# A transformer block on one core: queries of the last two blocks with tokens on partitions, attention later, and small products and memsets ahead of the first real work

## The chip, the cores and the metric

The kernel runs on one core of a Trainium2 chip. The metric is device time in microseconds (us), as the median of several runs. A profile of one execution gives each instruction's start and duration; times in it count from the start of its span.

## The reference, cut to what matters

Input and output are 2048 tokens of 512 numbers in bf16.

```python
def _layernorm(x, axis=-1, eps=1e-5):
    ...
def _A_ref(x, wqkv, wo):                       # 32 heads of 16
    q, k, v = ...                              # x @ wqkv
    phi = lambda t: jnp.where(t > 0, t + 1, jnp.exp(t)) + 1e-6
    pq, pk = phi(q), phi(k)
    kv = jnp.einsum("bhsd,bhse->bhde", pk, v)
    z = jnp.einsum("bhsd->bhd", pk)
    num = jnp.einsum("bhqd,bhde->bhqe", pq, kv)
    den = jnp.einsum("bhqd,bhd->bhq", pq, z)[..., None] + 1e-6
    o = num / den
    return (...)(o).reshape(B, S, D) @ wo
def _B_ref(x, w1, w2):                         # w1: 512 x 1792, w2: 1792 x 512
    ...                                        # relu(x @ w1) @ w2
h = x + _A_ref(_layernorm(x, axis=-1), A_wqkv, A_wo)
h2 = h + _B_ref(_layernorm(h, axis=-1), B_w1, B_w2)
```

## The kernel before

The 2048 tokens are 16 tiles of 128 (t = 0 to 15), and four blocks of four tiles (c = 0 to 3). Nothing is looped: one list of words, `ORDER`, is walked from front to back, and each word calls a function `op_<name>` with the numbers behind it. So the list sets the order of the instructions on every engine; the framework adds the waits (an instruction that reads or overwrites what another wrote waits for that one's semaphore, also where both run on the same engine). All loads, transposes by DMA and stores are issued by SP, one after the other, over eight semaphores in turn.

The words that matter here:

- `lx`, `lk`, `lq`, `lv`, `lo`, `l1`, `l2`: loads of the input and of the weights. `const`, `masks`, `table`: constants, masks, ACT's function table.
- `S.t`, `A.t` (DVE): mean and variance of tile t, in two instructions (BN_STATS, BN_AGGR). `R.t.n` (ACT): the scale, as a logarithm and an exponential, for n tiles. `N.t` (DVE): the normalized tile.
- `T.t` (PE) and `E.t` (ACT): transpose of tiles 0 to 3 by PE, and its copy to `lnT`. `X.t` (SP): the same for the others by DMA.
- `K.t` (PE, four products): keys of a tile. `F`, `U` (ACT: exponential, relu), `M`, `D` (DVE: minimum, sum): the function phi on them. `W`, `qW`: sum and relu in one DVE instruction instead. `G.t` (PE, four products): the sum over tokens of the normalized tile times its keys, from which `kv` makes the state with the value weights `wv`; `m` multiplies it by `wo`.
- `za`, `zf`, `z`, `zc`, `zh`: z, the sum of the keys.
- `Q.c.j` (PE, four products): queries of a block with features on partitions, a quarter at a time; `qF`, `qU`, `qM`, `qD` the function phi.
- `dn.c` (PE, 16 products of 8 columns): the denominators of a block; `dnl`, `dnx` (ACT): their reciprocals, spread over 16 columns each; `dt` (DMA) or `rt` with `re`/`rv`: the transposes of those; `dm.c.j` (DVE): queries times reciprocals, into `pqs`.
- `h.t` (PE, four products) and `hD.t` (DVE): the attention's output and the residual sum; `s`, `a`, `r`, `n`, `x`/`t` with `e`: the second layer norm and its transpose.
- `p.c.f` (PE, four products, w1), `pA`/`pD` (relu on ACT or DVE, two f at a time, into `at`), `f.t` (PE, 14 products, w2), `fo.t` (DVE), `fd.t` (store): the second layer. A number in these words that names a bank is the PSUM bank written.
- `warm`, `warmf`: products of zeros, ahead of and between the first transposes.

Of the kernel before, what the change touches and what calls it, by code (L numbers as in the profile page):

```python
# [18 lines left out]
const lx.0.1 lx.1.1 warmf.4.3 warm.1.3 S.0 table A.0 R.0.1 S.1 lx.2.2 lk.0.2 warm.1.3 N.0 A.1 S.2 R.1.1 lk.2.2  # L19
lx.4.2 A.2 T.0.7 E.0 warm.1.3 S.3 R.2.1 K.0.1.0.2 lx.6.2 A.3 R.3.1 K.0.1.2.2 N.1 T.1.5 F.0.1 E.1 N.2 N.3 T.3.2  # L20
lx.8.4 E.3 S.4 S.5 A.4 T.2.5 lx.12.4 lq.0.2 A.5 K.1.0.0.2 R.4.2 S.6 M.0.1 N.5 S.7 N.4 X.5 E.2 U.0.1 D.0.1 K.3.7
K.1.0.2.2 F.3.1 M.3.1 X.4 K.2.3.0.2 U.3.1 A.7 A.6 K.2.3.2.2 U.1.1 R.6.2 F.2.1 F.1.1 G.0 D.3.1 G.3 S.9 U.2.1 N.7
N.6 S.8 K.5.1 K.4.0 M.2.1 A.8 A.9 R.8.2 U.4.2 M.1.1 X.7 D.2.1 F.4.2 D.1.1 N.9 S.12 X.6 N.8 X.9 G.2 K.7.3 S.13
A.12 A.13 G.1 R.12.2 K.6.2 K.9.1 M.4.2 S.10 F.6.2 N.12 D.4.2 S.11 A.10 U.6.2 X.8 M.6.2 N.13 G.4 X.12 K.8.0 A.11
R.10.2 S.14 D.6.2 G.5 G.6 X.13 N.10 N.11 S.15 F.8.2 M.8.2 X.11 A.15 U.8.2 A.14 D.8.2 R.14.2 G.7 za.2 za.4 K.12.0
G.9 K.13.1 N.15 N.14 X.10 lq.2.2 K.11.3 F.12.2 K.10.2 M.12.2 U.12.2 F.10.2 masks X.15 X.14 lv.0.2 lv.2.2 l1.0.2
U.10.2 za.6 D.12.2 M.10.2 G.8 za.8 D.10.2 Q.0.1.1 Q.0.0.0 qF.0.0.2 qU.0.0.2 za.10 G.12 K.14.2 K.15.3 Q.0.2.0
za.12 Q.0.3.1 G.13 F.14.2 G.11 qF.0.2.2 l2.10.4 qM.0.0.2 M.14.2 W.14.2 zf.12 G.10 qD.0.0.2 qM.0.2.2 G.14
# [28 lines left out]
def kernel(  # L57
# [10 lines left out]
    nc = tc.nc  # L68
# [45 lines left out]
    erep = const.tile([P, P], BF16, name="erep")  # L114
# [9 lines left out]
    z_sb = big.tile([P, KD], F32, name="z_sb")  # L124
    acts = [big.tile([P, KF, CW], BF16, name=f"at{i}") for i in range(2)]
# [15 lines left out]
    r4 = rd  # L141
# [19 lines left out]
    unit = {"k": 0, "q": NT}  # L161
# [49 lines left out]
    op_l2 = lambda k, n: load_d(w2_sb, w2_v, k, n)  # L211

# [139 lines left out]
    op_W = lambda t, n: relu_add_of("k", t, n)  # L352
    op_qF = lambda c, j, n: exp_of("q", c * KD + j, n)
# [23 lines left out]
    def op_z(jb, b, t0=0):  # L377
        at_bank["z"] = b
        parts = [pk(t)[:, 0, :] for t in range(t0, NT)] + [acts[1][:, i, :] for i in (4, 5) if t0]
        for i, part in enumerate(parts):  # L380
            nc.tensor.matmul(
                bk[:, b, jb : jb + 1], lhsT=part[:, jb * P : (jb + 1) * P], rhs=ones[:],
                start=(i == 0), stop=(i == len(parts) - 1),
            )
# [39 lines left out]
    def op_d4(c, b):  # L424
        at_bank["d4", c] = b
        for jb in range(KD):
            nc.tensor.matmul(
                bk[jb * Q4 : (jb + 1) * Q4, b, :], lhsT=zhd[:, jb, :], rhs=pqT[c][:, jb, :],
                start=True, stop=True,
            )  # L430

    def op_dl4(c):
        nc.scalar.activation(
            out=ld[:, c % 2, :], in_=bk[:, at_bank["d4", c], :], func=ACT.Ln, bias=eps6[:], scale=1.0
        )

    def op_dx4(c):
# [154 lines left out]
```

## Time and profile before

| | |
|---|---|
| median of three runs | 170.3 us (169.92 to 170.45) |
| span of the profiled execution | 168.8 us; its own device time is not listed beside it |
| PE / DVE / ACT busy | 163.1 / 104.4 / 65.1 us |
| bytes moved by DMA | 15.49 MB, 92 GB/s over the span |
| granted TensorE clock | 1.000 on the mean |

The span runs from the first to the last instruction, and the median of the runs is 1.5 us above it. In the rows, a line such as L237 is a line of the kernel, "x4" counts instructions merged into a row, and what stands in brackets is the idle time ahead and what ended it. The profile gives PE's matmuls with their length through the pipeline, so that neighbours overlap; what one costs is the distance from start to start.

### The profile page before, as it was taken

What the parts mean: (1) busy time and instruction counts of PE and PEld (TensorE: products, weight loads), DVE (VectorE), ACT (ScalarE), POOL (GpSimd) and SP (SyncE); (2) the same over time, 40 slices, a digit from 0 to 9 for tenths busy, and PEclk for the clock granted to TensorE, in tenths of its full rate; (3) what the DMA queues carried; (4) which work ended last, traced back from release to release, by engine and by line L of the source; (5) the groups of instructions that cost most, each with busy time, mean ns of one, the idle gap of its engine ahead of it and who ended that gap; (6) DMA issues with size and microseconds to landing.
All of it is one profiled execution on the core that took longest, in us unless ns stands there. A gap on an engine that the chain in (4) does not pass through costs nothing.

```text
span 168.8 us, 2286 instructions
## 1 busy us (share of the span) xinstructions
PE 163.1 (97%) x855; PEld 78.0 (46%) x871; DVE 104.4 (62%) x205; ACT 65.1 (39%) x97; POOL 4.8 (3%) x21
## 2 busy tenths in 40 slices
PE   7989999999999999999999999999999999999993
PEld 5344344445644454444444444444444444444553
DVE  3899998997668999699819879215102432050251
ACT  3698775875879947432000003004320420400000
POOL 7400000000000000000000000000000000000000
PEclk9999999999999999999999999999999999999999
DMA  4975575689533353534130015500320000002023
GB/s 112 352 245 97 97 66 124 176 270 378 174 64 65 77 138 87 134 62 95 37 62 0 31 31 122 126 4 0 62 93 0 31 0 4 0 0 93 0 65 94
DMA packets 30491, 15.49 MB, mean 92 GB/s; under 512 B 23184, under 2 KB 29328, under 8 KB 30480
## 3 DMA queue, kind: packets, MB, share of 16 engines
q1 hardware_dynamic: 30480, 15.34, 35.5%
q8 instruction: 7, 0.11, 0.3%
q14 instruction: 4, 0.03, 0.1%
HBM read 7.86 MB, written 2.10 MB: 59 GB/s over the span
## 4 chain that ended last, share of the span: by engine, by line
PE 85%; DVE 7%; DMA 4%; issue 1%; SPq 0%
PE bk L541 29%; PE bk L521 28%; PE bk L505 8%; PE bk L318 8%; PE bk L362 6%; PE bk L310 4%; DVE st L237 3%; DMA x_nat<-in_A_x_dram 2%; DMA lnT<-h_nat 2%; DVE h_nat L262 2%; PE bk L459 1%; DVE eb L335 1%; PE bk L403 1%; PE bk L415 1%; SPq L201 0%
## 5 line engine op out<-in xcount | busy, mean ns | idle before, releaser
L541 PE MATMUL bk<-w_sb,at 128*128 128x512 bf16 (+2 forms) x247 | 50.1, 355 | 0.3
L521 PE MATMUL bk<-lnT,w_sb 128*128 128x512 bf16 x219 | 50.0, 379 | 0.3
L527 ACT ACTIVATE at<-bk 128x1024 bf16<-128x1024 f32 x14 | 14.2, 1023 | 57.4 <-PE bk L521 57.4
L541 PEld LDWEIGHTS <-at 128*128 128x128 bf16 x252 | 23.6, 98 | 25.4 <-ACT at L527 0.3
L549 DVE SCALAR_TENSOR_TENSOR gT<-bk,rstd,h_nat 128x512 bf16<-128x512 f32 (+2 forms) x18 | 12.2, 689 | 35.7 <-PE bk L541 35.6
L521 PEld LDWEIGHTS <-w_sb 128*128 128x128 bf16 x224 | 21.8, 98 | 25.8
L532 DVE TENSOR_SCALAR at<-bk 128x1024 bf16<-128x1024 f32 x14 | 17.1, 1218 | 12.8 <-PE bk L521 12.6
L328 ACT ACTIVATE eb<-bk 128x1024 bf16<-128x1024 f32 (+1 forms) x18 | 16.6, 928 | 6.6 <-PE bk L310 4.8
L310 PE MATMUL bk<-wk_sb,lnT 128*128 128x512 bf16 x63 | 15.3, 380 | 0.4 <-ACT lnT L291 0.3
L505 PE MATMUL bk<-m_sb,pqs 128*128 128x512 bf16 x63 | 15.4, 380 | 0.1
L318 PE MATMUL bk<-lnT,wq_sb 128*128 128x512 bf16 x61 | 15.1, 379 | 0.1
L362 PE MATMUL bk<-at,h_nat 128*128 128x512 bf16 x55 | 13.5, 379 | 0.1
L331 ACT ACTIVATE rb<-bk 128x1024 bf16<-128x1024 f32 (+1 forms) x14 | 12.5, 904 | 0.3 <-PE bk L310 0.3
L511 DVE TENSOR_TENSOR h_nat<-bk,x_nat 128x512 bf16<-128x512 f32 x16 | 10.5, 680 | 2.9 <-PE bk L505 2.9
L237 DVE BATCH_NORM_STATS2 st<-x_nat 128x6 f32<-128x512 bf16 x16 | 10.8, 680 | 2.4 <-DMA x_nat<-in_A_x_dram 2.4
L239 DVE BATCH_NORM_STATS2 st<-h_nat 128x6 f32<-128x512 bf16 x16 | 10.7, 683 | 0.1
L310 PEld LDWEIGHTS <-lnT 128*128 128x128 bf16 x64 | 6.0, 98 | 8.4 <-ACT lnT L291 1.0
L362 PEld LDWEIGHTS <-h_nat 128*128 128x128 bf16 x64 | 6.2, 98 | 7.4 <-issue 0.2
L505 PEld LDWEIGHTS <-pqs 128*128 128x128 bf16 x64 | 5.9, 98 | 7.9 <-DVE pqs L495 1.8
L318 PEld LDWEIGHTS <-wq_sb 128*128 128x128 bf16 x64 | 5.9, 98 | 6.4
L472 ACT ACTIVATE wk_sb<-ld 128x1024 bf16<-128x1024 f32 x8 | 8.1, 1050 | 0.1
L335 DVE TENSOR_SCALAR eb<-eb 128x1024 bf16<-128x1024 bf16 (+1 forms) x18 | 6.8, 383 | 0.9 <-ACT eb L328 0.9
(63 smaller groups left out, 93.5 us busy)
## 6 DMA issues: line engine op xcount, KB each, us to landing
out_dram<-gT SPq DMA_DIRECT2D x15, 128.0 KB, 1.9
w_sb<-in_B_w_dram SPq DMA_DIRECT2D x2, 896.0 KB, 9.8
x_nat<-in_A_x_dram SPq DMA_DIRECT2D x2, 512.0 KB, 6.3
w_sb<-in_B_w_dram SPq DMA_DIRECT2D x2, 512.0 KB, 9.5
x_nat<-in_A_x_dram SPq DMA_DIRECT2D x3, 256.0 KB, 4.6
w_sb<-in_B_w_dram SPq DMA_DIRECT2D x2, 384.0 KB, 3.5
wk_sb<-in_A_wqkv_dram SPq DMA_DIRECT2D x2, 256.0 KB, 4.3
wq_sb<-in_A_wqkv_dram SPq DMA_DIRECT2D x2, 256.0 KB, 4.9
```

Source lines behind the costliest of these rows:

```text
L237: op_S = lambda t: nc.vector.bn_stats(out=st[:, t, :], in_=x_nat[:, t, :])
L310: nc.tensor.matmul(bk[:, b, :], lhsT=lnT[c][:, kd, j * P : (j + 1) * P], rhs=wk_sb[:, kd, :], start=(kd == 0), stop=(kd == KD - 1),)
L318: nc.tensor.matmul(bk[:, b, :], lhsT=wq_sb[:, kd, j * P : (j + 1) * P], rhs=lnT[c][:, kd, :], start=(kd == 0), stop=(kd == KD - 1),)
L328: nc.scalar.activation(out=buf(eb, kind, i, n), in_=bank(at_bank[kind, i], n), func=ACT.Exp)
L331: nc.scalar.activation(out=buf(rb, kind, i, n), in_=bank(at_bank[kind, i], n), func=ACT.Relu)
L362: nc.tensor.matmul(bk[:, KD + kd, :], lhsT=ln_nat[:, t, kd * P : (kd + 1) * P], rhs=pk(t)[:, 0, :], start=(t == 0), stop=(t == NT - 1),)
L505: nc.tensor.matmul(bk[:, b, :], lhsT=pqs[:, (c * KD + jb) % NQ, j * P : (j + 1) * P], rhs=m_sb[:, jb, :], start=(jb == 0), stop=(jb == KD ...
L521: nc.tensor.matmul(bk[:, b, cols], lhsT=w1_sb[:, kd, f * P : (f + 1) * P], rhs=lnT[c][:, kd, cols], start=(kd == 0), stop=(kd == KD - 1),)
L527: nc.scalar.activation(out=acts[c % 2][:, f : f + n, :], in_=bank(at_bank["p", c, f], n), func=ACT.Relu)
L532: nc.vector.tensor_scalar(out=acts[c % 2][:, f : f + n, :], in0=bank(at_bank["p", c, f], n), scalar1=0.0, scalar2=None, op0=ALU.max,)
L541: nc.tensor.matmul(bk[:, b, 0 : w * P], lhsT=acts[c % 2][:, f, j * P : (j + 1) * P], rhs=w2_sb[:, f, k * P : (k + w) * P], start=(f == 0), ...
L549: nc.vector.scalar_tensor_tensor(out=o_t[:, t % NO, cols], in0=bk[:, at_bank["f", t, k], 0 : w * P], scalar=rstd2[:, t : t + 1], in1=h_nat ...
```

## The change

The queries of tiles 8 to 15 (blocks 2 and 3) are now made with tokens on partitions (`Y.t`, 4 products each; `yF`, `yU`, `yM`, `yD` for phi). For them the denominators come from DVE: z is spread to all partitions by four products of 128 columns with ones (`zd` on DVE, `zr` on PE, `zC` on ACT), `dT` multiplies two tiles by it into an f32 tile, `dR` adds up 16 columns at a time; `dl`, `dx` (ACT) make the reciprocals, `dy` (DVE) multiplies, and `ty` (DMA) transposes into `pqs`. Their `h` products come later, between the first `f` and `p.1`. Four of the `p.0` blocks are computed in two halves of 256 columns.

At the start, `warmf` is replaced by `warms.70`, seventy products of 64 columns, and 40 memsets of one column of a new tile `pad` (`idle.24`, then twice `idle.8`) stand on DVE. The loads up to `lq` head the list, `masks` comes ahead of `const`, and loads of `w2` are spread among the transposes. The mask `erep` and unused functions go.

```diff
-const lx.0.1 lx.1.1 warmf.4.3 warm.1.3 S.0 table A.0 R.0.1 S.1 lx.2.2 lk.0.2 warm.1.3 N.0 A.1 S.2 R.1.1 lk.2.2
+lx.0.1 lx.1.1 lx.2.2 lk.0.2 lk.2.2 lx.4.2 lx.6.2 lx.8.4 lx.12.4 lq.0.2 table masks const S.0 A.0 S.1 R.0.1 A.1 N.0 S.3
+idle.24 R.1.1 S.2 A.3 A.2 N.1 R.3.1 N.3 R.2.1 N.2 S.5 idle.8 idle.8 S.4 A.5 A.4 warms.70.2 T.0.3 warm.1.4 warm.1.7
+T.1.0 T.3.4 warm.1.5 E.0 E.1 E.3 R.4.2 T.2.5 K.0.7.0.2 K.0.7.2.2 K.1.3.0.2 K.3.0 F.0.1 E.2 K.1.3.2.2 K.2.2.0.2
...
+    pad = const.tile([P, 1], F32, name="pad")
-    ones = const.tile([P, 1], BF16, name="ones")
+    ones = const.tile([P, P], BF16, name="ones")
...
+    def op_idle(n):
+        for _ in range(n):
+            nc.vector.memset(pad[:], 0.0)
...
+    def op_Y(t, b):
+        c, j = divmod(t, CT)
+        at_bank["y", t] = b
+        for kd in range(KD):
+            nc.tensor.matmul(
+                bk[:, b, :], lhsT=lnT[c][:, kd, j * P : (j + 1) * P], rhs=wq_sb[:, kd, :],
+                start=(kd == 0), stop=(kd == KD - 1),
+            )
...
+    def op_zr(b):
+        at_bank["zr"] = b
         for jb in range(KD):
             nc.tensor.matmul(
...
+                bk[:, b, jb * P : (jb + 1) * P], lhsT=ones[:], rhs=zdg[:, jb, :], start=True, stop=True
+            )
...
+    def op_dT(t, n):
+        nc.vector.tensor_tensor(
+            out=prod[:, 0:n, :], in0=toks(t, n), in1=zrep.broadcast_to([P, n, D]), op=ALU.mult
+        )
+
+    def op_dR(t, n):
+        nc.vector.tensor_reduce(
+            out=den[:, t * H : (t + n) * H], in_=prod[:, 0:n, :].rearrange("p t (h r) -> p (t h) r", r=DH),
+            axis=mybir.AxisListType.X, op=ALU.add,
+        )
...
+    def op_dy(t, n):
+        nc.vector.tensor_tensor(out=toks(t, n), in0=toks(t, n), in1=rn[:, t % CT : t % CT + n, :], op=ALU.mult)
...
+    def op_ty(t):
+        nc.sync.dma_start_transpose(out=pqs_of(t), in_=toks(t, 1)[:, 0, :])
```

What this makes of the order shows at three places. First DVE at the start, before: from the normalization of tile 0 (L262) to the statistics of tiles 2 and 3 (L237, L238) and on to the normalizations of tiles 1 to 3. The brackets name the semaphores an instruction waits for; DVE_49 is DVE's own.

```order
L262 TENSOR_SCALAR h_nat<-x_nat,mv,rstd 128x512 [waits DVE_49,Activation_49]
L238 BN_AGGR mv<-st 128x2 [waits DVE_49]
L237 BN_STATS st<-x_nat 128x6 [waits DMAHW2_49]
L238 BN_AGGR mv<-st 128x2 [waits DVE_49]
L237 BN_STATS st<-x_nat 128x6
L238 BN_AGGR mv<-st 128x2 [waits DVE_49]
L262 TENSOR_SCALAR h_nat<-x_nat,mv,rstd 128x512 [waits Activation_49] x2
```

And after, from the same normalization (now L264) through tile 3's statistics (L239), the memsets (L213) and tile 2's statistics to tile 5's and the second row of memsets:

```order
L264 TENSOR_SCALAR h_nat<-x_nat,mv,rstd 128x512 [waits Activation_49]
L239 BN_STATS st<-x_nat 128x6 [waits DMAHW2_49]
L213 MEMSET pad 128x1
L213 MEMSET pad 128x1 [waits DVE_49] x23
L239 BN_STATS st<-x_nat 128x6
L240 BN_AGGR mv<-st 128x2
L240 BN_AGGR mv<-st 128x2 [waits DVE_49]
L264 TENSOR_SCALAR h_nat<-x_nat,mv,rstd 128x512 [waits Activation_49]
L264 TENSOR_SCALAR h_nat<-x_nat,mv,rstd 128x512 [waits DVE_49,Activation_49] x2
L239 BN_STATS st<-x_nat 128x6 [waits DMAHW5_49]
L213 MEMSET pad 128x1
L213 MEMSET pad 128x1 [waits DVE_49] x15
```

The second statistics of the pair now stand behind 24 memsets, of which 23 wait for DVE's own semaphore, and those of tile 4 behind 16.

Second, ACT at the start, before: the scales (L243, L244) of tiles 0 and 1, the copy of tile 0's transpose (L291), the scales of tiles 2 and 3, the exponential of tile 0's keys (L328) and the copies of the other two.

```order
L243 ACTIVATE rstd<-mv,eps_73 128x1 [waits DVE_49]
L244 ACTIVATE rstd<-rstd 128x1 [waits Activation_49]
L291 ACTIVATE lnT_81<-bk 128x4x128 [waits PE_49]
L243 ACTIVATE rstd<-mv,eps_73 128x1 [waits DVE_49]
L244 ACTIVATE rstd<-rstd 128x1 [waits Activation_49]
L243 ACTIVATE rstd<-mv,eps_73 128x1 [waits DVE_49]
L244 ACTIVATE rstd<-rstd 128x1 [waits Activation_49]
L328 ACTIVATE eb<-bk 128x512 [waits PE_49]
L291 ACTIVATE lnT_81<-bk 128x4x128 [waits PE_49] x2
```

And after, from the scale of tile 3 on (L245, L246; copies L293, exponential L339):

```order
L245 ACTIVATE rstd<-mv,eps_73 128x1 [waits DVE_49]
L246 ACTIVATE rstd<-rstd 128x1 [waits Activation_49]
L245 ACTIVATE rstd<-mv,eps_73 128x1 [waits DVE_49]
L246 ACTIVATE rstd<-rstd 128x1 [waits Activation_49]
L293 ACTIVATE lnT_81<-bk 128x4x128 [waits PE_49] x3
L245 ACTIVATE rstd<-mv,eps_73 128x2 [waits DVE_49]
L246 ACTIVATE rstd<-rstd 128x2 [waits Activation_49]
L339 ACTIVATE eb<-bk 128x512 [waits PE_49]
L293 ACTIVATE lnT_81<-bk 128x4x128
```

The copy of tile 0 moved behind the scales of tiles 3 and 2, and the scale of tiles 4 and 5 ahead of the first exponential and of tile 2's copy.

Third, DVE in the middle, where the first `f` products follow the first `p`. Before: an eviction of p into `at` (L532), aggregates, the product of block 2's queries with the reciprocals (L495), the next eviction.

```order
L532 TENSOR_SCALAR at_94<-bk 128x1024
L240 BN_AGGR mv_102<-st_101 128x2
L495 TENSOR_TENSOR pqs<-pqT_87,rd 128x1024 x2
L532 TENSOR_SCALAR at_94<-bk 128x1024
L239 BN_STATS st_101<-h_nat 128x6
L511 TENSOR_TENSOR h_nat<-bk,x_nat 128x512
```

And after (evictions L576, `dT` L460, `dR` L465, the minimum L346):

```order
L576 TENSOR_SCALAR at_98<-bk 128x1024
L460 TENSOR_TENSOR prod<-pqT_87,zrep 128x1024
L576 TENSOR_SCALAR at_98<-bk 128x1024
L465 TENSOR_REDUCE den<-prod 128x64
L576 TENSOR_SCALAR at_98<-bk 128x1024
L346 TENSOR_SCALAR eb<-eb 128x1024
L460 TENSOR_TENSOR prod<-pqT_87,zrep 128x1024
L465 TENSOR_REDUCE den<-prod 128x64
```

The multiplications and sums for the denominators now stand between the evictions that free the banks for p and f.

More of the change, by code (lines that the diff above doesn't have):

```diff
@@ L24 @@
[L24 to L28, printed above, removed]
@@ L421, in op_mD, with op_zd @@
         nc.vector.tensor_copy(out=m_sb[:, jb : jb + n, :], in_=bank(at_bank["m", jb], n))
-    def op_d4(c, b):
-        at_bank["d4", c] = b
+    def op_zd():
+        nc.vector.tensor_tensor(
+            out=zdg[:], in0=ident.rearrange("p (o n) -> p o n", o=1).broadcast_to([P, KD, P]), in1=z_on(P),
+            op=ALU.mult,
+        )
+    def op_zr(b):
+        at_bank["zr"] = b
         for jb in range(KD):
             nc.tensor.matmul(
-                bk[jb * Q4 : (jb + 1) * Q4, b, :], lhsT=zhd[:, jb, :], rhs=pqT[c][:, jb, :],
-                start=True, stop=True,
-            )
@@ L432, in op_dl4, with op_zC, toks @@
-    def op_dl4(c):
+                bk[:, b, jb * P : (jb + 1) * P], lhsT=ones[:], rhs=zdg[:, jb, :], start=True, stop=True
+            )
+    def op_zC():
+        nc.scalar.activation(out=zrep[:], in_=bank(at_bank["zr"]), func=ACT.Copy)
+    def toks(t, n):
+        return pqT[t // CT][:, t % CT : t % CT + n, :]
+    def op_dT(t, n):
+        nc.vector.tensor_tensor(
+            out=prod[:, 0:n, :], in0=toks(t, n), in1=zrep.broadcast_to([P, n, D]), op=ALU.mult
[5 more added lines that the diff above has]
+        )
@@ L433, in op_dl4, with op_dl, op_dx @@
+    def op_dl(t, n):
+        cols = den[:, t * H : (t + n) * H]
+        nc.scalar.activation(out=cols, in_=cols, func=ACT.Ln, bias=eps6[:], scale=1.0)
+    def op_dx(t, n):
+        src = den[:, t * H : (t + n) * H].rearrange("p (h o) -> p h o", o=1)
         nc.scalar.activation(
-            out=ld[:, c % 2, :], in_=bk[:, at_bank["d4", c], :], func=ACT.Ln, bias=eps6[:], scale=1.0
-        )
-    def op_dx4(c):
-        nc.scalar.activation(out=r4[:, c, :], in_=ld[:, c % 2, :], func=ACT.Exp, scale=-1.0)
@@ L440, in op_rp @@
-    def op_rp(c, jb, b):
-        at_bank["rp", c, jb] = b
-        rows = slice(jb * Q4, (jb + 1) * Q4)
-        nc.tensor.matmul(
-            bk[:, b, :], lhsT=erep[rows, :], rhs=r4[rows, c, :], start=True, stop=True
-        )
-    def op_rm(c, jb, n):
-        i = (c * KD + jb) % NQ
-        nc.vector.tensor_tensor(
-            out=pqs[:, i : i + n, :], in0=bank(at_bank["rp", c, jb], n), in1=pqT[c][:, jb : jb + n, :],
-            op=ALU.mult,
-        )
+            out=rn[:, t % CT : t % CT + n, :].rearrange("p t (h r) -> p (t h) r", r=DH),
@@ L454, in op_dn, with op_rE @@
+    def op_rE(t):
+        nc.scalar.activation(out=pqs_of(t), in_=at_bank["ry", t], func=ACT.Copy)
     def op_dn(c, b):
```

86 lines of the change are left out of this document (49 added, 37 removed).

## The prediction

> **What bounds the kernel now.** I read the page first, then the chain of work that ended last, then the timelines of PE, ACT and DVE over the first 24 us. "Product" below is one PE matmul with 512 columns.
>
> The page's first part and three groups of its fifth:
>
> ```profile
> span 168.8 us, 2286 instructions
> PE 163.1 (97%) x855; PEld 78.0 (46%) x871; DVE 104.4 (62%) x205; ACT 65.1 (39%) x97; POOL 4.8 (3%) x21
> ...
> L459 PE MATMUL bk<-zhd,pqT 128*128 128x8 bf16 x64 | 2.2, 166 | 0.0
> L369 DVE TENSOR_TENSOR at<-at,at 128x1024 f32<-128x1024 f32 x5 | 6.1, 1223 | 0.1
> L338 DVE TENSOR_TENSOR pqT<-rb,eb 128x1024 bf16<-128x1024 bf16 x5 | 3.4, 688 | 0.1
> L343 DVE SCALAR_TENSOR_TENSOR pqT<-bk,eb 128x1024 bf16<-128x1024 f32 x3 | 3.7, 1221 | 0.1
> ```
>
> (The four group rows are from the view of groups that keeps shapes apart.) PE is busy for 97%, but its matmuls are pipelined, so spacing decides. The chain, in order of time:
>
> ```profile
> 17.65 3.40 DMA lnT<-h_nat
> 21.05 0.04 issue
> 21.10 1.04 PE bk L310 x4
> ...
> 41.53 0.38 PE bk L459 x16
> ...
> 42.79 0.89 PE bk L403 x16
> ...
> 44.55 0.22 PE bk L281 x4
> ...
> 71.70 2.00 PE bk L505 x8
> ...
> 129.81 10.14 PE bk L521 x47
> ...
> 166.16 0.03 issue
> 166.18 0.35 DVE gT L549
> ```
>
> 47 products in 10.14 us are 0.216 us each, and from 21.1 to 166.2 us the chain stays on PE. So a delay of PE before 21 us is not made good later: after it there is only work. The start:
>
> ```profile
> 1.24 3.78 PE L221 MATMUL bk<-m_sb 128*128 128x256 f32 x8 [1.24 <-DVE ones L177]
> 4.82 1.06 PE L215 MATMUL bk<-m_sb 128*128 128x512 bf16 x2
> 5.67 0.63 PE L281 MATMUL bk<-ident,h_nat 128*128 128x128 bf16 x4
> 6.10 0.63 PE L215 MATMUL bk<-m_sb 128*128 128x512 bf16 x1
> 6.99 1.05 PE L310 MATMUL bk<-wk_sb,lnT 128*128 128x512 bf16 x4 [0.26 <-ACT lnT L291]
> ...
> 9.43 2.75 PE L310 MATMUL bk<-wk_sb,lnT 128*128 128x512 bf16 x12
> 12.13 1.02 PE L362 MATMUL bk<-pk_lo,h_nat 128*128 128x512 bf16 x4
> ```
>
> The key products of tile 0 (K.0) start at 6.99. From 9.43 PE runs K.1, K.3 and K.2 without a pause, so K.2, the last four of the twelve, starts at 9.43 + 8 x 0.216 = 11.16, and G.0 at 12.13. Behind that lie two busy engines, first DVE, then ACT:
>
> ```profile
> 1.14 0.06 DVE L175 MEMSET eps<- 128x1 f32 x1
> 1.15 0.06 DVE L176 MEMSET eps<- 128x1 f32 x1
> ...
> 3.12 0.69 DVE L237 BATCH_NORM_STATS2 st<-x_nat 128x6 f32<-128x512 bf16 x1 [1.90 <-DMA x_nat<-in_A_x_dram]
> 3.85 0.18 DVE L238 BATCH_NORM_AGGREGATE mv<-st 128x2 f32<-128x6 f32 x1
> ...
> 5.60 0.70 DVE L237 BATCH_NORM_STATS2 st<-x_nat 128x6 f32<-128x512 bf16 x1 [0.47 <-DMA x_nat<-in_A_x_dram]
> 6.33 0.18 DVE L238 BATCH_NORM_AGGREGATE mv<-st 128x2 f32<-128x6 f32 x1
> ...
> 8.24 1.28 DVE L237 BATCH_NORM_STATS2 st<-x_nat 128x6 f32<-128x512 bf16 x2
> ```
>
> ```profile
> 6.83 0.28 ACT L243 ACTIVATE rstd<-mv,eps 128x1 f32<-128x1 f32 x1
> 7.15 0.20 ACT L244 ACTIVATE rstd<-rstd 128x1 f32<-128x1 f32 x1
> 7.34 0.29 ACT L243 ACTIVATE rstd<-mv,eps 128x1 f32<-128x1 f32 x1
> ...
> 8.57 1.08 ACT L291 ACTIVATE lnT<-bk 128x512 bf16<-128x512 bf16 x2
> ```
>
> Three things to see. Two statistics that do not wait for each other start 1.28 - 0.69 = 0.59 us apart (0.60 below). An aggregate that waits for the statistic before it on its own engine starts 0.03 to 0.04 us after that one's end (3.12 + 0.69 to 3.85; 5.60 + 0.70 to 6.33). And memsets of one column that wait for nothing start 0.01 us apart, though each lasts 0.06.
>
> **The change, part by part.** *The memsets.* All 40 write the same tile, and the order of instructions shows that 23 of the first 24 and 15 of the 16 after them wait for DVE's own semaphore. No row shows a memset that waits. The low bound is 0.01 us each (the rows at 1.14 and 1.15), the high one 0.06 + 0.035 = 0.095 (its length, and the gap of the waiting aggregate). I take 0.095, since those are the instructions with the same kind of wait: 23 x 0.095 + 0.01 = 2.20 us and 15 x 0.095 + 0.01 = 1.43, together 3.63; by the low bound 0.40. Queued behind them on DVE are S.2 and S.4, and behind those ACT, which now has the scales of tiles 2 and 3 ahead of the copies E.0, E.1, E.3, and the scale R.4 ahead of F.0 and E.2.
>
> *The ramp, step by step*, with ACT's starts as its rows have them (logarithm to exponential 0.32, that to the next logarithm 0.19; a copy or exponential of 512 every 0.49). S.3 starts at 5.60, with the load, as before. Memsets from 6.20; S.2 at 8.40; A.2 at 9.13, ended 9.31. ACT: R.3 9.21, R.2 9.73, E.0 10.17, E.1 10.66, E.3 11.15, free at 11.64. DVE: N.1, N.3, N.2 as their scales come, N.2 at 10.30; S.5 10.62; memsets from 11.22; S.4 12.65; A.4 13.38, ended 13.55. ACT: R.4 13.58, F.0 14.02, E.2 14.51, ended about 15.10. So K.2 starts at 15.15 instead of 11.16, and the sixteen products ahead of its end are the same as before. G.0 waits for D.0: DVE runs S.6, N.4, N.5, S.7, M.0, A.7, A.6 and D.0 from 13.46, D.0 ends at 16.2, and G.0 starts at 16.24 instead of 12.13: **4.11 us late**, of which 3.63 are the memsets and 0.48 the order.
>
> *The 70 small products* have no row. They lie between the 0.023 us of the products of 8 columns (16 in 0.38) and the 0.11 of transposes at the slow clock (4 in about 0.43, from 5.67 to 6.10): 1.6 to 7.7 us from about 1.1. The end, 8.8 at worst, is ahead of T.1, which waits for N.1 (9.23 + 0.4): nothing. If the memsets were cheap, N.1 would come at 7.4 and the worst end would cost 1.4. The four f32 products removed cost nothing before either: T.0 followed them at 5.67.
>
> *Products of 8 columns*: two of four groups go, 2 x 0.38 = -0.76 us on PE. The four sums for all partitions (128 columns) add 0.22, as the four transposes at 44.55. PE: **-0.54**. Y and Q are equally many products (8 x 4 each); four of the p blocks are cut in halves with the same columns in all.
>
> *Late attention.* Before, eight h products at 71.70 take 2.00 us where 8 x 0.216 = 1.73 are work; tiles 8 and 9 no longer stand there: **-0.25**. What is late next is DVE. It gains four multiplications into f32 and four reductions of 1024. The reductions have no row: 1.22 us (the f32 row of 1024) as the low end, 1.36 as the other (0.68 for 512 in the statistics, twice). Three fused adds of 1.22 become adds of 0.69 (-1.6), two evictions of 1.22 come over from ACT, and the multiplications by the reciprocal are as many as before. Sum: 4 x 1.22 + 4 x 1.29 - 1.6 + 2.4 = +10.8 us. It has room where tiles 8 to 15 stood:
>
> ```profile
> 60.00:80.00 20.00, 19.89 (x121) 9.31 (x123) 17.89 (x31) 9.60 (x13) 0.00 (x0) 1.00 0.46 106
> 80.00:100.00 20.00, 19.89 (x92) 9.11 (x93) 14.42 (x32) 0.50 (x2) 0.00 (x0) 1.00 0.13 27
> ```
>
> 7.7 us are free there (DVE is the third figure), and eight tiles' eviction, statistics and centring move behind 90 us. It is tight ahead of f.2, whose bank the eviction pD.0.8 frees, behind the first of these multiplications and reductions: I take **+0.2**, between 0 and 0.8 (four reductions at 1.36 instead of 1.22, and as much again).
>
> *Loads and masks.* Transposes by DMA stay 41. POOL's mask for the removed helper goes, and the identity stands behind the masks, ready before T.0: nothing. wv's second half now lands behind 2.8 MB. At the 265 GB/s of 30 to 40 us below that is 10.6 us from about 34, so 44.6; the products that need it started at 42.79 and move past 46. Hidden, with 1.6 us to spare.
>
> ```profile
> 30.00:40.00 10.00, 9.95 (x54) 4.66 (x54) 9.65 (x14) 6.03 (x7) 0.00 (x0) 1.00 0.87 265
> ```
>
> **Sum:** 4.11 - 0.54 - 0.25 + 0.2 = +3.5 us. The span goes from 168.8 to 172.3; the median of the runs, 170.3, lies 1.5 above the span, and I keep that: **173.8 us**. In general the change is -0.1 us + 39 x the price of a waiting memset; a measurement of this kernel can tell about 0.3%, or 0.5 us.
>
> **The rule that speaks against it.** On the granted clock the windows above say 1.00 in every stretch, yet the two products at 4.82 start (1.06 - 0.63) = 0.43 apart, and the four at 6.99 at 0.22: PE is at half speed until about 7. In the changed kernel PE has nothing between its last warming product (about 6.5) and T.1 (about 9.6). The Trainium skill (TensorE: Matmul & The Clock Gate, "Why this matters for your kernels") says to leave no gap over about 3 us between bursts, or the clock halves again. By that rule the products from T.1 on would run slow once more; no row of before has such a gap, so the trace neither bears it out nor denies it.
>
> **The rivals.** *Cheap memsets (not slower).* If a wait on the engine's own semaphore costs nothing where the work is one column, each memset is 0.01 us: -0.1 + 0.4 = +0.3, **170.6**. For it: the rows at 1.14 and 1.15. Against: both gaps ahead of the waiting aggregates. It decides below 0.016 us each (0.6 / 39), where the change is under 0.5 us. Chance 0.12 (no change 0.08, faster 0.04, the latter if the 0.2 and part of the order's 0.48 vanish as well).
>
> *The clock falls back.* T.1 to K.2 at 0.43 a product instead of 0.216: K.0 starts at 11.4 and the sixteen products end at 18.3 instead of 16.0, +2.1 at G.0 if the slow speed lasts all through; if it ends 5.75 us after the first work, as before (1.24 to 6.99), at about 15.4, then +0.7. So 174.5 to 175.9, **175.2**. For it: the gap of 3.1 us; against: 1.5 us of it fall into the wait for E.2 anyway. Chance 0.12.
>
> *DVE becomes the bound in late attention.* If a reduction of 1024 takes 2.2 us rather than 1.3, four of them put 3.6 us ahead of the evictions that feed the first f products: up to **177.4**. Against: no DVE row of 1024 lasts over 1.23. Chance 0.06.
>
> **How the numbers follow.** The forecast has 0.70, its own range 172.4 (a memset at 0.06) to 174.8. Of the rest the cheap memsets lie below and the third rival above; with the clock's bounds the range is 171.8 to 175.8. Slower: 0.70 + 0.12 + 0.06 = 0.88; same 0.08; faster 0.04.
>
> **What would show it.** Right: starts of the memsets 0.09 to 0.10 apart; S.2 near 8.4 and S.4 near 12.7; K.2 near 15.2 and G.0 near 16.2; from there PE at 0.216 a product. Wrong: memsets 0.01 to 0.06 apart; products 0.43 apart after 9.6; PE waiting between 76 and 100 us for L576 or L555's producers; the products with wv waiting for a DMA.

## The result: 175.2 us, 2.9% slower

The changed kernel takes 175.21 us on the median of four runs (174.66 to 175.41), the kernel before 170.19 beside it: a ratio of 1.0291, 95% interval 1.0269 to 1.0312, or 5.0 us. Its profiled execution took 174.66 us at a span of 172.9; the other three have spans of 173.4 to 173.7.

The page of the changed kernel, its first part and the row of the granted clock in 40 slices of 4.3 us:

```profile
span 172.9 us, 2427 instructions
PE 163.9 (95%) x904; PEld 80.8 (47%) x921; DVE 117.6 (68%) x255; ACT 66.4 (38%) x102; POOL 2.3 (1%) x12
...
PEclk9957999999999999999999999999999999999999
```

PE is as busy as before (163.1), in a span that is 4.1 us longer. The third and fourth slices, at 5 and 7 tenths of full speed, are new (the row of before is 9 throughout). DVE at the start, from its timeline:

```profile
5.18 0.69 DVE L239 BATCH_NORM_STATS2 st<-x_nat 128x6 f32<-128x512 bf16 x1
5.82 2.81 DVE L213 MEMSET pad<- 128x1 f32 x23
8.68 0.69 DVE L239 BATCH_NORM_STATS2 st<-x_nat 128x6 f32<-128x512 bf16 x1
8.70 0.06 DVE L213 MEMSET pad<- 128x1 f32 x1
...
10.79 0.69 DVE L239 BATCH_NORM_STATS2 st<-x_nat 128x6 f32<-128x512 bf16 x1
11.43 1.82 DVE L213 MEMSET pad<- 128x1 f32 x15
13.29 0.69 DVE L239 BATCH_NORM_STATS2 st<-x_nat 128x6 f32<-128x512 bf16 x1
13.31 0.06 DVE L213 MEMSET pad<- 128x1 f32 x1
```

From the first memset to the statistics queued behind it pass 8.68 - 5.82 = 2.86 us, and 13.29 - 11.43 = 1.86 us in the second row: 4.72 us in all. The starts of the single memsets (5.820, 5.946, 6.071, 6.197 and so on) are 0.1255 apart. The last memset of each row is recorded 0.02 us behind the start of the statistics. PE's timeline shows what that does:

```profile
1.25 3.76 PE L237 MATMUL bk<-m_sb 128*128 128x64 bf16 x70 [1.25 <-DVE m_sb L177]
5.33 0.40 PE L283 MATMUL bk<-ident,h_nat 128*128 128x128 bf16 x4 [0.31 <-DVE h_nat L264]
5.78 0.38 PE L217 MATMUL bk<-m_sb 128*128 128x512 bf16 x1
9.94 1.19 PE L283 MATMUL bk<-ident,h_nat 128*128 128x128 bf16 x8 [3.78 <-DVE h_nat L264]
...
11.77 5.19 PE L312 MATMUL bk<-wk_sb,lnT 128*128 128x512 bf16 x16
16.90 1.02 PE L378 MATMUL bk<-pk_lo,h_nat 128*128 128x512 bf16 x4
```

PE has nothing for 3.78 us, the transposes of tiles 1 and 3 start at 9.94, and G.0 starts at 16.90 instead of 12.13. It starts 0.05 us after DVE has the sum D.0 that it waits for (16.42 + 0.43 = 16.85):

```profile
16.42 0.43 DVE L349 TENSOR_TENSOR pk_lo<-rb,eb 128x512 bf16<-128x512 bf16 x1
```

In the chain of work that ended last, DVE (with a few scales on ACT) now stands until 42 us, where before PE stood from 21 on:

```profile
40.79 1.13 DVE at L385
42.89 1.89 PE bk L378 x8
```

Both are close there: PE is busy for 24.89 of the 25 us from 15 to 40, the last row of the next view. The granted clock, from the view by stretches (the first figure behind the stretch is its length; PEclk is the third figure from the end):

```profile
0.00:8.00 8.00, 4.54 (x75) 3.98 (x76) 3.96 (x28) 2.28 (x5) 2.30 (x12) 1.00 0.68 205
8.00:15.00 7.00, 5.07 (x21) 2.54 (x22) 5.46 (x35) 3.08 (x10) 0.00 (x0) 0.51 0.48 181
15.00:40.00 25.00, 24.89 (x114) 11.18 (x115) 24.21 (x57) 19.21 (x33) 0.00 (x0) 1.00 0.73 183
```

The trace's clock events place the half clock at 8.11 to 14.94, that is 6.83 us or two stretches of 3.413. The Trainium skill (TensorE: Matmul & The Clock Gate, "What's actually happening") gives the gate a free-running window of 3413 ns; this trace agrees on the length (3.413 us).

### The profile page after: what moved, and what is told of

It is laid out like the page before. It is cut to its first block, busy times and chain, and to the rows that moved or that the text cites. A ratio compares the mean times of both kernels' runs of the same rounds, so it can differ in the third digit from the quotient of the medians.

```text
span 172.9 us, 2427 instructions
## 1 busy us (share of the span) xinstructions
PE 163.9 (95%) x904; PEld 80.8 (47%) x921; DVE 117.6 (68%) x255; ACT 66.4 (38%) x102; POOL 2.3 (1%) x12
## 4 chain that ended last, share of the span: by engine, by line
PE 64%; DVE 21%; ACT 6%; issue 4%; DMA 3%; SPq 1%; DVEq 0%; ACTq 0%
PE bk L565 28%; PE bk L585 28%; PE bk L549 6%; DVE st L239 5%; DVE at L385 4%; DVE h_nat L264 3%; DVE eb L346 2%; DVE at L349 2%; ACT eb L339 2%; DVE pad L213 1%; DMA x_nat<-in_A_x_dram 1%; DMA rd<-wk_sb 1%; DVE pqs L539 1%; ACT wk_sb L516 1%; SPq L535 1%
## 5 line engine op out<-in xcount | busy, mean ns | idle before, releaser
L565 PE MATMUL bk<-lnT,w_sb 128*128 128x512 bf16 (+1 forms) x236 | 49.6, 365 | 0.2
L565 PEld LDWEIGHTS <-w_sb 128*128 128x128 bf16 x240 | 23.4, 98 | 24.7
L576 DVE TENSOR_SCALAR at<-bk 128x1024 bf16<-128x1024 f32 x16 | 19.3, 1217 | 17.1 <-PE bk L565 17.1
L571 ACT ACTIVATE at<-bk 128x1024 bf16<-128x1024 f32 x12 | 12.1, 1017 | 47.7 <-PE bk L565 47.7
L339 ACT ACTIVATE eb<-bk 128x1024 bf16<-128x1024 f32 (+1 forms) x18 | 16.8, 931 | 4.4 <-PE bk L312 2.4
L312 PE MATMUL bk<-wk_sb,lnT 128*128 128x512 bf16 x63 | 16.5, 409 | 0.1
L342 ACT ACTIVATE rb<-bk 128x1024 bf16<-128x1024 f32 (+1 forms) x17 | 15.1, 921 | 0.0
L239 DVE BATCH_NORM_STATS2 st<-x_nat 128x6 f32<-128x512 bf16 x16 | 10.8, 683 | 2.0 <-DMA x_nat<-in_A_x_dram 1.9
L312 PEld LDWEIGHTS <-lnT 128*128 128x128 bf16 x64 | 6.6, 105 | 8.6 <-issue 2.1
L245 ACT ACTIVATE rstd<-mv,eps 128x2 f32<-128x2 f32 (+2 forms) x14 | 4.1, 294 | 9.9 <-DVE mv L240 9.9
L329 PE MATMUL bk<-wq_sb,lnT 128*128 128x512 bf16 x31 | 7.7, 379 | 0.1
L320 PE MATMUL bk<-lnT,wq_sb 128*128 128x512 bf16 x31 | 7.3, 379 | 0.1
L346 DVE TENSOR_SCALAR eb<-eb 128x1024 bf16<-128x1024 bf16 (+1 forms) x18 | 6.9, 386 | 0.0
```

What stands on the lines that cost most here:

```text
L239: op_S = lambda t: nc.vector.bn_stats(out=st[:, t, :], in_=x_nat[:, t, :])
L312: nc.tensor.matmul(bk[:, b, :], lhsT=lnT[c][:, kd, j * P : (j + 1) * P], rhs=wk_sb[:, kd, :], start=(kd == 0), stop=(kd == KD - 1),)
L339: nc.scalar.activation(out=buf(eb, kind, i, n), in_=bank(at_bank[kind, i], n), func=ACT.Exp)
L342: nc.scalar.activation(out=buf(rb, kind, i, n), in_=bank(at_bank[kind, i], n), func=ACT.Relu)
L565: nc.tensor.matmul(bk[:, b, cols], lhsT=w1_sb[:, kd, f * P : (f + 1) * P], rhs=lnT[c][:, kd, cols], start=(kd == 0), stop=(kd == KD - 1),)
L571: nc.scalar.activation(out=acts[c % 2][:, f : f + n, :], in_=bank(at_bank["p", c, f], n), func=ACT.Relu)
```

## The experiments

Each was timed beside the kernel before on the same chip; a ratio is to that. Device time lies 1.7 to 1.9 us above the span in all of them but two, of which more below.

**No memsets.** `idle.24` and both `idle.8` are taken out.

```diff
-idle.24 R.1.1 S.2 A.3 A.2 N.1 R.3.1 N.3 R.2.1 N.2 S.5 idle.8 idle.8 S.4 A.5 A.4 warms.70.2 T.0.3 warm.1.4 warm.1.7
+R.1.1 S.2 A.3 A.2 N.1 R.3.1 N.3 R.2.1 N.2 S.5 S.4 A.5 A.4 warms.70.2 T.0.3 warm.1.4 warm.1.7
```

> The changed kernel without its 40 memsets, all else as it is. If the waiting memsets are the cause (2.86 us from 5.82 to 8.68 and 1.86 us from 11.43 to 13.29 on DVE in the profile of the changed kernel), the ramp shortens by about 4.7 us: G.0 near 12.3 instead of 16.90, span near 168.3, time near 170.2, the same as before. If the rest of the change costs as well (late attention, the order of the scales), it stays above 171.

Measured: 170.72 us (170.01 to 172.42 in ten runs), ratio 1.0047 [1.0016, 1.0079]. Of the 5.0 us over the kernel before, 0.7 are left; the time lies between the 170.2 expected and the 171 that would have meant a cost elsewhere. What is left shows on PE:

```profile
11.99 1.02 PE L378 MATMUL bk<-pk_lo,h_nat 128*128 128x512 bf16 x4
13.69 1.04 PE L312 MATMUL bk<-wk_sb,lnT 128*128 128x512 bf16 x4 [0.68 <-ACT eb L339]
```

G.0 is 0.14 earlier than in the kernel before, but the keys of tile 4 then wait 0.68 us. ACT is named, but what comes last is tile 4's transpose by DMA: SP issues it at 10.31, that issue takes 2.15 us where most take 1.2, and the tile lands 3.3 us after its start.

**Each memset its own column.** The same 40 memsets, without a wait on each other.

```diff
-    pad = const.tile([P, 1], F32, name="pad")
+    pad = const.tile([P, 40], F32, name="pad")
...
-            nc.vector.memset(pad[:], 0.0)
+            k = at_bank["pad"] = at_bank.get("pad", -1) + 1
+            nc.vector.memset(pad[:, k : k + 1], 0.0)
```

> The changed kernel with the same 40 memsets, each into a column of its own, so that none waits for the one before it. If the wait sets the price, 40 x 0.01 us remain: time 170.3 to 170.8, G.0 near 12.7. If the price is that of 40 more instructions on DVE (issue, or moved instruction fetches), it stays near 175.2.

Measured: 171.55 us, 1.0077 [1.0052, 1.0102]. DVE's timeline:

```profile
6.03 0.34 DVE L214 MEMSET pad<- 128x1 f32 x23
...
9.09 0.23 DVE L214 MEMSET pad<- 128x1 f32 x15
```

0.013 us each: the price of a memset in the changed kernel is the wait, not the work. The time lies above the 170.3 to 170.8 expected, 0.8 us above the kernel without memsets, and the two rows together are only 0.5 us long (6.03 to 6.33 and 9.09 to 9.28). Half clock stands here too, in one window:

```profile
8.50:12.00 3.50, 3.50 (x14) 1.55 (x12) 3.47 (x25) 2.53 (x8) 0.00 (x0) 0.51 0.71 269
```

Here it does hold up G.0. DVE has the sum ready at 12.63 + 0.43 = 13.06, but PE works without a pause from 9.07 and comes to G.0 at 13.98:

```profile
12.63 0.43 DVE L350 TENSOR_TENSOR pk_lo<-rb,eb 128x512 bf16<-128x512 bf16 x1
```

```profile
9.07 5.07 PE L313 MATMUL bk<-wk_sb,lnT 128*128 128x512 bf16 x16
13.98 1.03 PE L379 MATMUL bk<-pk_lo,h_nat 128*128 128x512 bf16 x4
```

How the 0.8 us divide between the clock and the two rows isn't settled.

**The gap filled.** Ten more warming products keep PE busy while it waits for tile 1; the memsets stay.

```diff
-warm.1.7
+warm.11.7
```

> The changed kernel with ten more warming products of 512 columns in PE's gap between the last warming product and T.1 (5.78 to 9.94), so that the clock has no idle stretch to fall back on. If DVE's chain sets the ramp, the clock stays at 1 and the time falls by 0 to 0.8 us only (174.4 to 175.2; G.0 still near 16.9). If the halved clock from 8.1 to 14.9 us is the cause, it falls by 2 to 3.4 us (half of 6.8): 172 to 173.

Measured: 174.19 us (174.14 to 174.23), 1.0245 [1.0230, 1.0260]; the granted clock is 1.00 from 8 to 15 us. PE:

```profile
11.08 2.75 PE L312 MATMUL bk<-wk_sb,lnT 128*128 128x512 bf16 x12
15.67 1.04 PE L312 MATMUL bk<-wk_sb,lnT 128*128 128x512 bf16 x4 [1.84 <-ACT lnT L293]
16.79 1.02 PE L378 MATMUL bk<-pk_lo,h_nat 128*128 128x512 bf16 x4
```

At full speed twelve products end 1.84 us before tile 2's copy, and G.0 starts only 0.11 us earlier than with half the clock: DVE's and ACT's chain sets the ramp. The median is 1.0 us lower all the same, a little more than the 0 to 0.8 expected of this case and half or less of what the clock as the cause would have given. In the profiled executions another 0.27 us come at 62.5 us (the attention's products start 0.38 earlier), where SP's issues of the transposed reciprocals take less, the first row from the changed kernel, the second from this one:

```profile
56.21 2.88 SPq L535 DMA_TRANSPOSE rd<-wk_sb  x2
```

```profile
56.09 2.50 SPq L535 DMA_TRANSPOSE rd<-wk_sb  x2
```

**The memsets alone, in the kernel before.**

```diff
-... E.0 warm.1.3 S.3 R.2.1 ... E.3 S.4 S.5 A.4 ...
+... E.0 warm.1.3 idle.24 S.3 R.2.1 ... E.3 S.4 idle.16 S.5 A.4 ...
```

> The kernel before with the waiting memsets alone: 24 between the statistics of tiles 2 and 3, 16 between those of tiles 4 and 5. If they are the cause by themselves, it loses 4 to 5 us: 174.3 to 175.2, with G.0 near 16.5 instead of 12.13. If the loss needs the new order or late attention, under 2 us: below 172.3.

Measured: 174.22 us, 1.0252 [1.0235, 1.0268]: the memsets alone make the old kernel 4.2 us slower, 0.1 below the range expected, with G.0 at 16.89. DVE's two rows, then G.0 on PE:

```profile
6.39 2.83 DVE L216 MEMSET pad<- 128x1 f32 x23
...
11.73 1.81 DVE L216 MEMSET pad<- 128x1 f32 x15
```

```profile
16.89 1.02 PE L367 MATMUL bk<-pk_lo,h_nat 128*128 128x512 bf16 x4 [0.25 <-DVE pk_lo L343]
```

The clock is halved here as well, from 12.09 to 15.51, but G.0 waits 0.25 us for DVE, so DVE's chain sets its start.

**The 24 alone, and the 16 alone**, each in the changed kernel with the other row taken out.

> The changed kernel with the first 24 memsets alone. If each row of waiting memsets lies on the path with its whole length, it costs 23 x 0.1255 = 2.9 us over the kernel without memsets (170.72): 173.2 to 173.8. If only the second row matters (R.4 ahead of F.0 and E.2), it stays near 171.

> The changed kernel with the second 16 memsets alone. By whole lengths 15 x 0.1255 = 1.9 us over 170.72: 172.3 to 172.9. If the first row hides it or PE has work to spare there, under 171.5.

Measured: 174.01 us, 1.0231 [1.0206, 1.0255], and 172.08 us, 1.0141 [1.0105, 1.0176]. Both lie 0.2 us outside the ranges expected, the first above and the second below. Over the kernel without memsets that is 3.3 and 1.4, and 170.7 + 3.3 + 1.4 = 175.4, the changed kernel within 0.2. The costs are not just the lengths of the rows, though. The first row is 2.86 us long and costs more; the clock is halved in that run from 9.72 to 13.13, and what this adds isn't settled. The second is 1.86 us long and costs 0.5 less: without memsets the keys of tile 4 wait 0.68 us for their transposed tile, and with the 16 alone they follow G.0 at once (14.44, then 15.37), so that wait is hidden behind the row.

**The gap filled, without memsets.** Three more warming products (`warm.1.7` to `warm.4.7`).

> The changed kernel without memsets, and with three more warming products in what is left of the gap ahead of T.1 (6.13 to 6.92). If the spread of the kernel without memsets (170.01 to 172.42) and its 0.7 us over the kernel before are the clock, 169.9 to 170.2 with a small spread; if they are K.4's wait for its transposed tile (0.68 us at 13.69), the median stays at 170.5 to 170.9.

Measured: 170.70 us (170.52 to 171.21), 1.0047 [1.0029, 1.0064], clock 1.00. So the clock isn't what these kernels have over the one before. The wait of tile 4's keys has shrunk from 0.68 to 0.24 us, and the median hasn't moved, so that wait isn't the whole of it either.

**The old ramp with the new rest.** The old kernel's words up to `G.3` (two of them a place earlier, in part other banks), without memsets, then the changed kernel's.

```diff
-lx.0.1 lx.1.1 lx.2.2 ... idle.24 ... warms.70.2 ... G.0 ... G.3
+const lx.0.1 lx.1.1 warmf.4.3 warm.1.3 S.0 table A.0 ... X.4 X.5 E.2 U.0.1 D.0.1 ... G.0 D.3.1 G.3
```

> The changed kernel with the start of the kernel before (const, warmf, the early copy E.0, no memsets, no small products) up to G.3, then the changed order. PE has 0.54 us less to do than before and no h products of tiles 8 and 9 that wait (0.25): if late attention and the queries with tokens on partitions are hidden, 169.2 to 169.8, faster than before; if DVE's added 10.8 us come onto the path, 170.5 to 172.

Measured: 171.17 us, 1.0074 [1.0052, 1.0096]; the expectation missed. The ramp is the old one (G.0 at 11.89), but PE then waits for transposes:

```profile
21.31 1.90 PE L315 MATMUL bk<-wk_sb,lnT 128*128 128x512 bf16 x8 [0.41 <-DMA lnT<-h_nat]
...
25.68 3.63 PE L315 MATMUL bk<-wk_sb,lnT 128*128 128x512 bf16 x16 [0.74 <-DMA lnT<-h_nat]
```

**Loads behind the transposes**, first with the old ramp, then with the new one without memsets and with the gap filled. Both get the same edit:

```diff
-... G.4 l2.0.3 X.9 X.8 lq.2.2 X.13 X.12 ... X.10 X.11 ... l2.10.4 X.15 X.14 ... l1.2.2
+... G.4 X.9 X.8 X.13 X.12 ... X.10 X.11 lq.2.2 ... X.15 X.14 ... l1.2.2 l2.10.4 l2.0.3
```

> The kernel of the early ramp (e5: the start of the kernel before, no memsets, the rest of the changed kernel), with the three loads that stand among the transposes by DMA moved: the load of w2 behind tile 7's transpose and the one behind tile 11's go to the end of the loads, the second half of wq goes behind the transposes of tiles 10 and 11, as in the kernel before. Theory (loads between the transposes on SP's queue hold up the transposed tiles): in e5 PE waited 1.2 us for them, of which the kernel before has next to nothing; those waits vanish, the span goes from 169.2 to 168.0 to 168.4, the median from 171.2 to 169.6 to 170.2, at the kernel before or up to 0.3% under it (late attention and DVE's denominators give the 0.6 us that PE has less to do). Rival (the transposes are late for another cause, such as the load of x behind them or DVE's normalizations): the waits stay at 1 us or more and the median at 170.8 to 171.4.

> The changed kernel without the memsets and with three more warming products in the gap (e8), with the same three loads moved out from among the transposes. Theory: here the ramp's order (the tile 4 products waiting 0.6 us for their transpose, which is ahead of all three loads) costs the 0.7 us that e8 has over the kernel before, so the loads change little: median 170.3 to 170.7. Rival: the loads among the transposes cost as much here as in e5, then the median falls by 0.8 to 1.2 us to 169.5 to 169.9.

Measured: 170.60 us, 1.0021 [1.0004, 1.0038], and 170.47 us, 1.0025 [1.0005, 1.0044]. With the old ramp the span fell as the theory said, from 169.2 to 168.1, but the median by half of that, to a value between theory and rival. The new ramp stays within its theory (170.3 to 170.7); what the 0.3 to 0.7 us are that the new ramp without memsets has over the kernel before isn't settled. In the two kernels with the old ramp, and in no other, the device time is scattered: 1.7 to 2.1 us above the span with the loads left in place, 1.7 to 2.9 with the loads moved. One row of the page stands out in both, that of the queue on which PE's instructions are fetched, a block of 16 KB at a time (packets, MB; here with the loads moved). Every other kernel has seven packets there:

```profile
q8 instruction: 6, 0.10, 0.3%
```

The trace's record of transfers has the seventh at 169.06 us, after the span's end at 168.1 (with the loads in place at 170.17, after 169.2).

**The fetches moved**, in the kernel just shown and in the kernel before:

```diff
-const lx.0.1 lx.1.1 warmf.4.3 warm.1.3
+const lx.0.1 lx.1.1 warms.70.3 warm.1.3
```

> The kernel of e9 (early ramp, loads behind the transposes) with the first f32 warming products replaced by the seventy products of 64 columns, as the change does. They take as long (3.8 us) but are more instructions, so all later instruction fetches of PE come earlier. In e9 and e5 the last of PE's seven fetches lies after the last work (169.1 and 170.2 us, spans 168.1 and 169.2), and in those two kernels alone the device time is scattered, 1.7 to 2.9 us above the span; in all others it is 1.7 to 1.9. Theory: the late fetch keeps the program from ending; here it comes near 155 us, the time is 1.7 to 1.8 above the span in every run, the median falls from 170.6 to 170.0 to 170.2. Rival (the scatter has another cause): offsets as in e9, median 170.4 to 170.8.

> The kernel before with its first f32 warming products replaced by the seventy products of 64 columns, nothing else. Its last fetch of PE's instructions moves from 162.9 us to near 150, inside the span in both. Theory: a fetch inside the span costs nothing, wherever it lies: 169.9 to 170.3, ratio 0.998 to 1.002, offset of time and span 1.7 as before. Rival: fetches cost by where they fall, then the span changes by 0.3 us or more and PE shows a gap at one of them.

Measured: 170.34 us, 1.0019 [1.0005, 1.0032], and 171.10 us, 1.0071 [1.0055, 1.0087].

In the first the last fetch comes at 152.5 us, and all twelve runs lie 1.67 to 1.78 above their span: the scatter went with the fetch behind the end. The median fell to between what theory and rival gave, and is still 0.2% above the kernel before, since the spans rose (167.9 to 169.2; the kernel before has 168.0 to 168.6 in the runs beside it).

In the second the theory fell and the rival held: one word, which takes 3.9 us on PE as its predecessor took 3.8, makes the old kernel 1.1 us slower. The first of the seven fetches moves from 22.85 to 10.48 us, the third from 63.6 to 51.5; the other instruction queue, with 8 KB packets, has its first inside the span at 19.64 instead of 19.53, so the 16 KB queue is PE's. G.0 is where it was (12.17). The loss begins at the transposes of the reciprocals, on SP, the kernel before first:

```profile
50.99 3.81 SPq L491 DMA_TRANSPOSE rd<-wk_sb  x3
```

```profile
51.00 4.80 SPq L491 DMA_TRANSPOSE rd<-wk_sb  x3
```

The first of the three is issued at the same time in both, but takes 2.18 us instead of 1.19. From 51 to 53.2 us the second kernel's DMA queues show one packet of instructions, and in the kernel before none:

```profile
q8 instruction: 1, 0.02, 3.5%
```

That fetch starts at 51.52. DVE, then PE, wait for it:

```profile
57.14 1.29 DVE L495 TENSOR_TENSOR pqs<-pqT,rd 128x1024 bf16<-128x1024 bf16 x2 [0.96 <-DMA rd<-wk_sb]
```

```profile
57.89 0.99 PE L505 MATMUL bk<-m_sb,pqs 128*128 128x512 bf16 x3 [0.40 <-DVE pqs L495]
```

Product by product, the second kernel is 0.23 us ahead on PE from 51 to 57 us (its issue at 46.53 took 1.39 us, that of the kernel before 1.76) and 0.67 behind from 62 to 71: this fetch costs 0.9 us. It catches up 0.27 at 71.6, since there the kernel before has a fetch of its own to bear: its issue at 63.30 takes 1.69 us, with a fetch at 63.60, and its counterpart at 63.97 takes 1.19. At the end 0.6 are left (spans 169.4 and 168.8). The other 0.5 of the 1.1 don't show in these two traces; the profiled execution of the kernel before was longer than the runs timed beside this experiment (168.0 to 168.6).

## Why the prediction was right, and where it was off

*The place was right.* S.2 and S.4 behind the memsets, ACT and PE behind them, nothing made good later: with the memsets out, 0.7 of the 5.0 us are left, and put alone into the old kernel they cost 4.2.

*The price was off.* The term of a waiting memset was 0.095 us, with 0.06 and 0.095 as bounds; it measured 0.1255, above both. Its length is 0.059, so the wake-up took 0.066 where the aggregate's gap of 0.035 was used. 2.20 + 1.43 = 3.63 measured 2.86 + 1.86 = 4.72, +1.09. With 0.1255 the prediction's own formula gives -0.1 + 39 x 0.1255 = +4.8, or 175.1 us (it counts 39 waiting memsets where the order has 38; with 38 it is 175.0). This term is the step that was off: of the kinds of wait with a row, the aggregate's was taken for the memset's, and 0.095 for the upper bound as well.

*What was luck.* The 175.2 us measured lie above the forecast's own range, 172.4 to 174.8. They lie in the whole range (to 175.8) only because the clock rival had widened it, and they equal that rival's price to the digit, though in the profiled run DVE's chain and not the clock set G.0. Of the signs listed, S.2 at 8.68, S.4 at 13.29 and G.0 at 16.90 came 0.3 to 0.7 us behind their places, the memsets 0.1255 apart instead of 0.09 to 0.10; and a sign of being wrong, products 0.43 apart after 9.6, did show.

*The ramp.* S.3 was put at 5.60 "as before" and came at 5.18, 0.42 earlier, because its load landed earlier. So G.0 is 4.77 late and not 4.11: +1.09 - 0.42 leaves 0.67, and the difference is 0.66. The seventy small products took 3.76 us, within 1.6 to 7.7, and cost nothing: the transpose of tile 0 waited for DVE.

*After G.0.* From G.0 to the span's end pass 172.9 - 16.90 = 156.0 us, before 168.8 - 12.13 = 156.7: -0.7, where -0.54 - 0.25 + 0.2 = -0.6 stood. The reductions lie at the low end:

```profile
L460 DVE TENSOR_TENSOR prod<-pqT,zrep 128x1024 f32<-128x1024 bf16 x4 | 4.9, 1220 | 0.1
L465 DVE TENSOR_REDUCE den<-prod 128x64 f32<-128x1024 f32 x4 | 4.9, 1214 | 0.1
```

The -0.25 of late attention was there in the trace, but tiles 8 and 9 were not its only cause: the wait at 71.62 stands behind the issue that a fetch lengthened at 63.30, and with the fetches moved the old order catches up 0.27 us there. PE shows no gap between 76 and 100 us, and no product waits for wv. Whether the 0.7 is a gain of the change isn't settled: the profiled execution of before, at 168.8, was itself longer than most of its runs (168.0 to 168.6 in the runs beside the last experiment), and the kernel with the old ramp, moved loads and moved fetches, which has all of the new middle, is at 1.0019 [1.0005, 1.0032] of the kernel before, so no gain shows there.

*From span to time.* 1.5 us were added; the profiled run has 1.76. In every run with both figures on record it is 1.66 or more, so 1.5 came of setting a long profiled execution beside the median of other runs. Then the other three runs have spans 0.5 to 0.8 longer than the profiled one. 173.8 + 0.6 (span 172.9 instead of 172.3) + 0.26 + 0.55 (median over profiled run) = 175.2.

*The rivals.* Cheap memsets: not so while they write one tile; without the wait they are cheap (0.013). DVE as the bound: the reductions took 1.21 us and not 2.2. The clock: it did fall, so the Trainium skill's rule (TensorE: Matmul & The Clock Gate, "Why this matters for your kernels") held for the gap of 3.78 us, and the products from 11.77 on were 0.427 apart until 14.75. But in the profiled run it cost 0.1 us at G.0, since the 1.84 us that PE would otherwise have waited for tile 2's copy (the kernel with the gap filled shows them) took it up; the point against this rival had put 1.5 us there. That it is so small here is due to DVE's chain: with a column for each memset, where the chain is shorter, G.0 came up to 0.9 us late by the clock (13.98 for 13.06). How much of the 1.0 us that the filled gap saves on the median is the clock isn't settled: the ten products move PE's fetches as well.

*What no step had:* the instruction fetches. The prediction put the small products down as nothing beside DVE's wait, and did not ask where in the program the fetches would then come.

## What to carry to other kernels

An instruction that rewrites what its own engine's last instruction wrote pays a wait; price a row of such instructions by rows of the same kind of wait, and keep the upper bound open, because a wake-up behind a short instruction can be longer than behind another. Before adding or taking away instructions anywhere, look at where the fetches of the instruction queue then fall: in this case one that fell on a DMA transpose which PE waited for cost 0.9 us far from the edit, and with one behind the last work some runs were 1 us longer. And judge a stall by what is late behind it: half the clock for 6.8 us moved G.0 by 0.1 us in the profiled run while another engine set the pace, and half of that time at half clock moved it by up to 0.9 where PE did.

## What the runs showed of the hardware

*A fetch of instructions lengthens the issue of a DMA transpose on SP.* Over all fourteen kernels of this case, the 470 issues with no fetch from 1.2 us ahead of their start to their end took 1.19 to 1.29 us; of the other 104, 35 took over 1.30. It matters where the fetch falls. In 19 issues a fetch of PE's (16 KB) began in their first 0.71 us, and all 19 took 1.45 to 2.18 us. With one that began ahead of the issue or later in it they took 1.19 to 1.48, and with only an 8 KB fetch of the other queue 1.19 to 1.76. Six of the 19, and one issue with no fetch near:

| kernel | issue at | took | fetch at |
|---|---|---|---|
| no memsets, tile 4's transpose | 10.31 | 2.15 | 11.02 |
| no memsets, gap filled, the same | 10.50 | 1.71 | 10.82 |
| kernel before, reciprocals | 63.30 | 1.69 | 63.60 |
| changed kernel, reciprocals | 56.21 | 1.57 | 56.35 |
| old ramp, loads moved, a tile's transpose | 22.25 | 1.71 | 22.42 |
| the same with fetches moved | 22.37 | 1.19 | none near |
| kernel before, fetches moved, reciprocals | 51.00 | 2.18 | 51.52 |

Only the last row comes from an edit that moves little else; for the others it is a reading of traces. Such an issue costs nothing where its tile isn't waited for: with the gap filled one at 72.87 took 2.15 us, and PE shows no wait behind it. PE itself showed no gap at a fetch. The Trainium skill (Runtime: NRT & Kernel Launch, "Instruction fetch mechanics") calls the cost of such a block mostly hidden; for PE that agrees, for SP's transposes 1.0 us in the last row does not.

*A fetch behind the last work goes with a longer and scattered time.* In the two kernels with six fetches inside the span the time lay 1.7 to 2.9 us above it, in all others 1.7 to 1.9, and moving the fetch inside ended it. That the program waits for such a fetch is the reading that fits; the traces don't show the wait itself, and the profiled run with the fetch at 169.06 lay only 1.86 us above its span.

*The clock* was halved for one stretch of 3.413 us where PE's longest wait ahead of it was 3.50 us (the 24 alone), 2.83 (the memsets in the kernel before) or 1.67 (own columns), and for two where it was 3.78 (the changed kernel). The length of the wait alone doesn't decide it: with the gap filled PE waited 1.84 us ahead of 15.67 and kept full speed. It also differs between executions: the four runs of the 16 alone have a mean granted clock of 1.0, 0.99, 0.989 and 1.0.
